# Last key chunk times values on 64x64 tiles, results by head, in a fused attention and mixer kernel

## The chip, the cores and the metric

The kernel runs on one core of a Trainium2 chip. The metric is the device time of one execution in microseconds. Before the change it is 580.24 us (median of three runs, 580.22 to 580.52).

## The reference, cut to what matters

```python
q_n = q / (norm(q) + 1e-6); k_n = k / (norm(k) + 1e-6)      # (8, 12, 448, 64)
scores = q_n @ k_n^T / tau                                   # tau = 0.1
attn = exp(scores) / sum(exp(scores))
x = (attn @ v), heads side by side                           # (8, 448, 768)
u = x + V^T (U^T x)                                          # rank 32, over the sequence
out = u + relu(u @ w_ch1) @ w_ch2                            # 768 -> 3072 -> 768
```

## The kernel before

Two heads form a pair, two pairs a couple; pair n = 6 b + p. Keys come in three chunks of 128 and a last one of 64. The last chunks of both heads of a pair share one tile of 128 rows. From n = 14 the kernel is in its steady state. A list of channel-mixer steps of the batch before ("fill") is spread between the parts of attention, so that TensorE (PE) never runs dry. One step is six matmuls, 0.98 us (second matrix, 384 columns) or 1.13 us (first matrix, 448 columns).

The product of the softmax numerators with the values, for half of the queries and both heads:

```python
def pe_V(b, p, half, bank):
    ...
    for i in range(2):                        # last chunk: both heads at once, 130 columns
        ic = 2 * half + i
        nc.tensor.matmul(out=av[:, i, :, :], lhsT=last_of(b, p)[:, ic * 128:(ic + 1) * 128],
                         rhs=vv[:, 2 * j:2 * j + 2, 3, :], start=(i == 0), stop=False, ...)
    for i in range(2):                        # three full chunks, head by head, 65 columns
        for h in range(2):
            for c in range(3):
                nc.tensor.matmul(out=av[:, i, h, :], lhsT=e[:, 2 * c + h, ...], rhs=vv[:, 2 * j + h, c, :], ...)
```

In the 130-column matmuls half of the products are with zeros: each head has its 64 keys in one half of the rows, and its values are zero in the other. Column 65 of the values is ones and gives the sum for the division on VectorE.

The steady loop (conditions that matter only outside it are left out), one turn for an even pair, one for the odd pair behind it; the number ahead of each part is its share of the fill put behind it:

```python
order = [                                                    # even n
    (2, lambda: (step_S3(*pairs[n]), Sc(n, 0, 1))),          # last-chunk scores of n and n+1, then chunks 0, 1
    (2, lambda: V(n - 1, 0)),
    (2, lambda: (V(n - 1, 1), X2(n - 1))),                   # X2: transposed copy of X by DMA
    (2, None),
    (3, lambda: (A2(n - 2), Sc(n, 2), Sc(n + 1, 0))),        # A2: U^T X of the couple n-2, n-1
    (2, False),
]
...
Sc(n, 1, 2)                                                  # odd n
H2(n - 3)                                                    # V (U^T X), added to the transposed X
...
order = [(2, lambda: V(n - 1, 0)), (2, None), (2, lambda: (V(n - 1, 1), X2(n - 1))), (2, None), (2, None)]
```

The result banks are two, `ps_av` and `ps_x`; the channel mixer has two more, `ps_m`, and the scores four: eight in all.

Of the kernel before, what the change touches and what calls it, by code (L numbers as in the profile page):

```python
# [9 lines left out]
FP = mybir.dt.float32  # L10
BF = mybir.dt.bfloat16
# [11 lines left out]
def kernel(  # L23
# [17 lines left out]
    nc = tc.nc  # L41

    B, H, S, D = q.shape
# [3 lines left out]
    NP = H // 2  # L47
    CC = C // 128
    NC = F // 128
    HC = C // 2  # L50
# [3 lines left out]
    work = ctx.enter_context(tc.tile_pool(name="work", bufs=2))  # L54
    psum = ctx.enter_context(tc.tile_pool(name="psum", bufs=1, space=bass.MemoryType.PSUM))
# [29 lines left out]
    est = Estimate()  # L85
# [24 lines left out]
    E, E3 = [], []  # L110
# [8 lines left out]
    def last_of(b, p):  # L119
        n = b * NP + p  # L120
        return E3[n // 2 % 2][:, n % 2, :]
# [63 lines left out]
    group_of = {}  # L185
# [30 lines left out]
    norm = {}  # L216
# [69 lines left out]
    FIRST4 = 2 * NP + 2  # L286
# [76 lines left out]

    X_of, av_of, A_of, up_of, XT_of = {}, {}, {}, {}, {}

    def pe_V(b, p, half, bank):
        gi, j = group_of[(b, p)]
        vv = norm[gi][1]
        e = E[(b * NP + p) % 2]
        if half == 0:  # L370
            X_of[(b, p)] = work.tile([128, 4, 128], BF, name="X", tag="X", bufs=2)
        av_of[(b, p, half)] = bank
        av = bank[:, 0:4 * (D + 1)].rearrange("p (i h d) -> p i h d", i=2, h=2)
        for i in range(2):
            ic = 2 * half + i
            nc.tensor.matmul(out=av[:, i, :, :], lhsT=last_of(b, p)[:, ic * 128:(ic + 1) * 128],  # L376
                             rhs=vv[:, 2 * j:2 * j + 2, 3, :],
                             start=(i == 0), stop=False, skip_group_check=True)
        for i in range(2):
# [3 lines that stand above are left out]
                    nc.tensor.matmul(out=av[:, i, h, :],  # L383
                                     lhsT=e[:, 2 * c + h, ic * 128:(ic + 1) * 128],
                                     rhs=vv[:, 2 * j + h, c, :],
                                     start=False, stop=(i == 1 and h == 1 and c == 2),
                                     skip_group_check=True)
        est.pe(0.52)
# [10 lines left out]
        est.dve(0.6)  # L399

    def step_V(b, p, half):
        if half == 1 and b * NP + p >= FIRST2:
            bank = psum.tile([128, 512], FP, name="up", tag="ps_x", bufs=1)
        else:
            bank = psum.tile([128, 512], FP, name="av", tag="ps_av", bufs=1)
        pe_V(b, p, half, bank)
        divide_V(b, p, half)
# [52 lines left out]
        XT_of[(b, p)] = t  # L460
        nc.sync.dma_start_transpose(out=t, in_=X_of[(b, p)].rearrange("p c d -> p (c d)"))

    def step_A2(b, p):
        ap = av_of[(b, p + 1, 1)][:, 384:512]
        for c in (0, 2):
            for i in range(2):
                for k in range(2):
                    r0 = 64 * i + 32 * k
                    nc.tensor.matmul(out=ap[r0:r0 + R, :], lhsT=U_sb[:, c + k, 0:R],  # L469
                                     rhs=X_of[(b, p + i)][:, c + k, :],  # L470
                                     start=False, stop=(c == 2), skip_group_check=True)
        A_of[(b, p)] = A_sb[(p // 2) % 2]
        nc.scalar.copy(out=A_of[(b, p)], in_=ap)  # L473
        est.pe(0.2)
        est.act(0.3)
# [16 lines left out]


    ut_of = {}

    def turn(b, half):

# [8 lines left out]
    def steps_m1(b):  # L506
        u = u_of(b)
        o = 64 if b % 2 == 0 else 0

        def one(f):  # L510
            mp = psum.tile([128, S], FP, name="mp", tag="ps_m", bufs=2)
            for cc in range(CC):
                nc.tensor.matmul(out=mp, lhsT=w1_sb[:, cc, f * 128:(f + 1) * 128],  # L513
                                 rhs=u[:, cc, 0:S], start=(cc == 0), stop=(cc == CC - 1))
            est.pe(1.13)
            if state_of["busy"] or est.act_first(0.55, 0.62):
                nc.scalar.activation(out=relu[:, f, o:o + S], in_=mp, func=AF.Relu)  # L517
            else:
                nc.vector.tensor_scalar_max(out=relu[:, f, o:o + S], in0=mp, scalar1=0.0)  # L519
            if b > 0 and f in (3, 12):  # L520
                turn(b, f // 12)

        return [lambda f=f: one(f) for f in range(NC)]

    def steps_m2(b):
        u = u_of(b)
        if b % 2 == 0:
            chunks = [(64 + 128 * c, 128 * c, c) for c in range(3)]
        else:
            chunks = [(384, 384, 3)] + [(128 * c, 128 * c, c) for c in range(3)]  # L530
        steps = []
        state = {}

        def part(half, ci, lo, hi, c0=0, c1=HC):
            r0, u0, c = chunks[ci]
            if lo == 0:
                state["mp"] = psum.tile([128, HC], FP, name="mp", tag="ps_m", bufs=2)
            mp = state["mp"][:, c0:c1]
            for f in range(lo, hi):
                nc.tensor.matmul(out=mp, lhsT=relu[:, f, r0:r0 + 128],  # L540
                                 rhs=w2_sb[:, f, half * HC + c0:half * HC + c1],
                                 start=(f == 0), stop=(b > 0 and f == NC - 1), skip_group_check=True)
            est.pe(0.0004 * (c1 - c0 + 6) * (hi - lo))
            if hi < NC:
                return
            o = work.tile([128, HC], FP, name="o_sb", tag="o_sb", bufs=3)[:, c0:c1]
            if b == 0:
                for i in range(3):
                    cc = half * 3 + i
                    nc.tensor.matmul(out=mp[:, i * 128:(i + 1) * 128], lhsT=u[:, cc, u0:u0 + 128],  # L550
                                     rhs=ident, start=False, stop=(i == 2), skip_group_check=True)
                est.pe(0.17)
                if est.act_first(0.48, 0.55):
                    nc.scalar.copy(out=o, in_=mp)
                else:
                    nc.vector.tensor_copy(out=o, in_=mp)
            else:
                nc.vector.tensor_add(o.rearrange("p (k d) -> p k d", d=128),  # L558
                                     mp.rearrange("p (k d) -> p k d", d=128),
                                     ut_of[(b, half)][:, c0 // 128:c1 // 128, c, :])  # L560
                est.dve(0.55)
            cols = slice(half * HC + c0, half * HC + c1)
            t4 = out[b, 0:256, cols].rearrange("(p c) d -> c p d", c=4)
            nc.sync.dma_start(out=t4[c], in_=o[0:64, :])
            if c < 3:
                t3 = out[b, 256:448, cols].rearrange("(p c) d -> c p d", c=3)
                other = nc.scalar if b == B - 1 and half == 1 else nc.sync
                other.dma_start(out=t3[c], in_=o[64:128, :])
            else:
                t4e = out[b - 1, 0:256, cols].rearrange("(p c) d -> c p d", c=4)  # L570
                nc.sync.dma_start(out=t4e[3], in_=o[64:128, :])

        for half in range(2):
            for ci in range(len(chunks)):
                if (b, half, ci) == (B - 1, 1, len(chunks) - 1):

                    for cs in ((0, 256), (256, 384)):
                        for i in range(2):
                            steps.append(lambda half=half, ci=ci, i=i, cs=cs:
                                         part(half, ci, 12 * i, 12 * i + 12, *cs))  # L580
                    continue
                for i in range(4):
                    steps.append(lambda half=half, ci=ci, i=i: part(half, ci, 6 * i, 6 * i + 6))
        return steps
# [4 lines left out]
    fill = []  # L589
# [22 lines left out]
    def Sc(n, *cs):  # L612
        step_S(*pairs[n], cs)

    def V(n, half):
        step_V(*pairs[n], half)
# [23 lines left out]
        M004 A5 red4q Ac5.a XT5 M104 H5 U5.a M045 M145 M205 red4k root4 M056 M156 R0 inv4 sc6q.v sc6k.v  # L640
        R1 M256 M306 R2 R3
    """
    bank1 = psum.tile([128, 512], FP, name="mp", tag="ps_m", bufs=2)
    spare = psum.tile([128, 512], FP, name="mp", tag="ps_m", bufs=2)
    copies = {"a": nc.scalar.copy, "v": nc.vector.tensor_copy}
    QK = {"q": 0, "k": 1}

# [149 lines left out]
    KEEP = 3  # L797
    for n in range(NP, NPAIR + 1):
# [38 lines left out]
        def X2(m):  # L837
            step_XT(*pairs[m])

        def A2(m):  # L840
            step_A2(*pairs[m])

        def H2(m):
            step_H2(*pairs[m])

        if n % 2 == 0:
            order = [
                (2, now and (lambda: (n >= FIRST4 and step_S3(*pairs[n]), Sc(n, 0, 1)))),
# [17 lines left out]
        if p == 1 and n - 2 > FIRST2:  # L866
            f(len(fill))
            fill.extend(steps_m1(b - 1) + steps_m2(b - 1))
        order = [
            (2, lambda: V(n - 1, 0)),  # L870
            (2, None if n > FIRST4 else (lambda: Sc(n, 3))),
            (2, lambda: (V(n - 1, 1), X2(n - 1))),
            (2, None),
            (2, None),
        ]
# [40 lines left out]
```

## Time and profile before

| | before |
|---|---|
| time | 580.24 us |
| span of the profiled run | 577.7 us |
| PE busy / chain of work that ended last | 98% / PE 95% |
| from the first last-chunk scores of n = 14 to the end ("the stretch") | 456.01 us |

The lines that carry the argument stand in the prediction. Most useful is a reading that no single view prints: the distance from one matmul's start to the next one's start. The ends of matmuls are modelled and overlap, but the starts add up to the time exactly.

### The profile page before, as it was taken

To read this page: it belongs to the slowest core of one execution; us is meant where nothing else is said; L and a number is where in the kernel's file an instruction comes from. 1 tells how busy PE (TensorE), PEld (TensorE's weight loads), DVE (VectorE), ACT (ScalarE), POOL (GpSimd) and SP (SyncE) were. 2 spreads that over 40 slices of the span, in tenths; PEclk is the share of its full clock that TensorE was granted. 3 is DMA by queue.
4 is the path that set the end of the run, shared out by engine and by line. 5 is a ranking of instruction groups with operands and counts; after the bars stand their busy time and mean duration, and the time that the engine had idled before them with its cause. 6 is when DMAs were issued, how large, how long until landed. Compare 5 with 4: busy or idle time off the path is not lost.

```text
span 577.7 us, 12301 instructions
## 1 busy us (share of the span) xinstructions
PE 568.7 (98%) x5098; PEld 329.3 (57%) x5098; DVE 211.8 (37%) x460; ACT 261.9 (45%) x449; POOL 213.8 (37%) x202
## 2 busy tenths in 40 slices
PE   7999999999999999999999999999999999999997
PEld 6665566555565556555555555655566555655565
DVE  6874552333342334423324333432244332320011
ACT  4877544555424653445324555246433374214300
POOL 8756574714416336416055064253261420000000
PEclk9999999999999999999999999999999999999999
DMA  6899999677467376575365663773654640231022
GB/s 166 192 249 239 235 209 213 181 144 138 104 149 176 81 142 136 134 142 111 91 159 146 113 137 99 148 174 83 128 131 113 132 74 16 54 71 36 6 50 57
DMA packets 139881, 74.52 MB, mean 129 GB/s; under 512 B 86688, under 2 KB 139696, under 8 KB 139824
## 3 DMA queue, kind: packets, MB, share of 16 engines
q1 hardware_dynamic: 129568, 63.20, 50.4%
q0 software_dynamic: 9632, 10.01, 10.2%
q8 instruction: 40, 0.66, 0.5%
q10 hardware_dynamic: 624, 0.51, 0.3%
q14 instruction: 17, 0.14, 0.1%
HBM read 52.19 MB, written 11.01 MB: 109 GB/s over the span
## 4 chain that ended last, share of the span: by engine, by line
PE 95%; DVE 1%; ACT 1%; SPq 1%; DMA 1%; issue 0%; DVEq 0%; ACTq 0%
PE mp L540 39%; PE mp L513 37%; PE sc L331 6%; PE av L383 3%; PE up L383 2%; PE av L376 1%; PE av L343 1%; PE tp L300 1%; PE sc L655 1%; PE up L376 1%; PE up L469 1%; DMA qst<-in_q_dram 1%; PE av L483 1%; ACT E L356 0%; PE sc L324 0%
## 5 line engine op out<-in xcount | busy, mean ns | idle before, releaser
L540 PE MATMUL mp<-w_sb,relu 128*128 128x384 bf16 (+2 forms) x1368 | 233.7, 323 | 0.0
L540 PEld LDWEIGHTS <-relu 128*128 128x128 bf16 x1368 | 126.7, 98 | 88.4 <-issue 13.1
L513 PEld LDWEIGHTS <-w_sb 128*128 128x128 bf16 x1128 | 105.1, 98 | 99.1 <-issue 9.7
L517 ACT ACTIVATE relu<-mp 128x448 bf16<-128x448 f32 x163 | 88.6, 543 | 128.3 <-PE mp L513 128.3
L356 ACT ACTIVATE E<-sc 128x896 bf16<-128x896 f32 x144 | 125.2, 923 | 21.7 <-PE sc L331 20.6
L268 POOL TENSOR_TENSOR qk<-kst,inv 128x512 bf16<-128x512 f32 x43 | 46.0, 1069 | 236.9 <-DVE inv L262 229.8
L513 PE MATMUL mp<-uO,w_sb 128*128 128x448 bf16 x576 | 114.2, 352 | 0.0
L513 PE MATMUL mp<-uE,w_sb 128*128 128x448 bf16 x552 | 112.9, 353 | 0.0
L558 DVE TENSOR_TENSOR o_sb<-mp,ut 128x384 f32<-128x384 f32 (+2 forms) x51 | 28.0, 549 | 141.0 <-PE mp L540 141.0
L248 DVE TENSOR_REDUCE ss<-sq 128x16 f32<-128x1024 f32 (+1 forms) x50 | 57.7, 1165 | 1.6 <-ACT sq L240 1.1
L268 POOL TENSOR_TENSOR qk<-qst,inv 128x512 bf16<-128x512 f32 x44 | 47.3, 1077 | 2.1 <-PE up L441 2.1
L383 PEld LDWEIGHTS <-E 128*128 128x128 bf16 x1152 | 45.0, 97 | 0.0
L519 DVE TENSOR_SCALAR relu<-mp 128x448 bf16<-128x448 f32 x25 | 15.6, 625 | 76.3 <-PE mp L513 75.8
L331 PE MATMUL sc<-qkT 64*64 64x448 bf16 x576 | 42.3, 359 | 0.6 <-ACT E L356 0.3
L243 POOL TENSOR_TENSOR sq<-kst 128x1024 f32<-128x1024 f32 (+1 forms) x23 | 42.6, 1855 | 0.2
L243 POOL TENSOR_TENSOR sq<-qst 128x1024 f32<-128x1024 f32 x21 | 39.9, 1899 | 7.3 <-DMA qst<-in_q_dram 7.3
L353 ACT ACTIVATE E<-av 128x448 bf16<-128x448 f32 x17 | 9.2, 541 | 47.3 <-PE up L343 47.3
L276 POOL CAST v<-vst 128x1024 bf16<-128x1024 f32 (+1 forms) x25 | 25.0, 1004 | 11.8 <-DMA vst<-in_v_dram 11.7
L383 PE MATMUL av<-v,E 128*128 128x65 bf16 x624 | 28.0, 193 | 0.0
L394 DVE RECIPROCAL rd<-av 128x4 f32<-128x4 f32 x52 | 9.3, 178 | 48.3 <-PE av L383 48.3
L473 ACT CAST A_sb<-up 128x128 bf16<-128x128 f32 x19 | 5.0, 263 | 47.6 <-PE up L469 47.6
L376 PEld LDWEIGHTS <-E 128*128 128x128 bf16 x192 | 18.0, 98 | 14.5 <-issue 0.8
(97 smaller groups left out, 347.8 us busy)
## 6 DMA issues: line engine op xcount, KB each, us to landing
out_dram<-o_sb SPq DMA_DIRECT2D x108, 96.0 KB, 2.2
w_sb<-in_moe_w_ch_dram POOLq DMA_DIRECT2D x8, 1152.0 KB, 18.4
qst<-in_q_dram SPq DMA_DIRECT2D x23, 256.0 KB, 3.9
vst<-in_v_dram SPq DMA_DIRECT2D x46, 128.0 KB, 3.0
kst<-in_k_dram SPq DMA_DIRECT2D x44, 128.0 KB, 2.8
qst<-in_q_dram SPq DMA_DIRECT2D x23, 192.0 KB, 3.9
vst<-in_v_dram SPq DMA_DIRECT2D x46, 96.0 KB, 2.8
kst<-in_k_dram SPq DMA_DIRECT2D x44, 96.0 KB, 2.7
```

The source lines that it names most:

```text
L243: nc.gpsimd.tensor_mul(sq[:, 0:self.nh * 4, :], self.flat(t), self.flat(t))
L248: nc.vector.reduce_sum(self.ss[:, j, 0:self.nh * 4], self.sq[j][:, 0:self.nh * 4, :], axis=AX.X)
L268: eng.tensor_mul(qks[self.gi % 2][:, j, i, :, :, :], t[:, 2 * j:2 * j + 2, :, :].rearrange("p h c d -> p c h d"), iv.unsqueeze(3).to_broad ...
L276: nc.gpsimd.tensor_copy(out=self.flat(v65[self.s])[:, :, 0:D], in_=self.flat(vst[self.s]))
L331: nc.tensor.matmul(out=sc[o:o + 64, h, 0:S], lhsT=t[r, 1, c * 128 + o:c * 128 + o + 64], rhs=t[r, 0, 0:S], start=True, stop=True)
L356: nc.scalar.activation(out=e[:, 2 * c:2 * c + 2, 0:S], in_=sc[:, :, 0:S], func=AF.Exp)
L376: nc.tensor.matmul(out=av[:, i, :, :], lhsT=last_of(b, p)[:, ic * 128:(ic + 1) * 128], rhs=vv[:, 2 * j:2 * j + 2, 3, :], start=(i == 0), s ...
L383: nc.tensor.matmul(out=av[:, i, h, :], lhsT=e[:, 2 * c + h, ic * 128:(ic + 1) * 128], rhs=vv[:, 2 * j + h, c, :], start=False, stop=(i == ...
L513: nc.tensor.matmul(out=mp, lhsT=w1_sb[:, cc, f * 128:(f + 1) * 128], rhs=u[:, cc, 0:S], start=(cc == 0), stop=(cc == CC - 1))
L517: nc.scalar.activation(out=relu[:, f, o:o + S], in_=mp, func=AF.Relu)
L540: nc.tensor.matmul(out=mp, lhsT=relu[:, f, r0:r0 + 128], rhs=w2_sb[:, f, half * HC + c0:half * HC + c1], start=(f == 0), stop=(b > 0 and f ...
L558: nc.vector.tensor_add(o.rearrange("p (k d) -> p k d", d=128), mp.rearrange("p (k d) -> p k d", d=128), ut_of[(b, half)][:, c0 // 128:c1 / ...
```

## The change

The intent: for even pairs, do the last chunk on four 64x64 tiles at once (two heads x two halves of each 128 queries), directly behind scores that use the same division of TensorE into tiles (the same "mode"). Results are kept by head, one bank each; the prediction says why. Both result banks are then taken at once, so U^T X moves to a bank of the channel mixer, and the even pair's products move up by a turn.

```diff
+    def open_V(b, p):
+        for h, (nm, tag) in enumerate((("av", "ps_av"), ("up", "ps_x"))):
+            av_of[(b, p, h)] = psum.tile([128, 512], FP, name=nm, tag=tag, bufs=1)
+        for ic in range(4):
+            for h in range(2):
+                r = slice(64 * h, 64 * h + 64)
+                for o in (0, 64):
+                    q0 = ic * 128 + o
+                    nc.tensor.matmul(out=av_of[(b, p, h)][o:o + 64, ic * (D + 1):(ic + 1) * (D + 1)],
+                                     lhsT=last_of(b, p)[r, q0:q0 + 64], rhs=vv[r, 2 * j + h, 3, :], ...)
+    def close_V(b, p, h):      # the 12 full-chunk products of one head, then its division
...
-        ap = av_of[(b, p + 1, 1)][:, 384:512]
+        ap = own_bank()[:, 0:128] if apart else av_of[(b, p + 1, 1)][:, 384:512]
...
+        if n % 2 == 0 and now and n >= FIRST4:
+            order = [
+                (3, lambda: (step_S3(*pairs[n]), Sc(n, 0, 1))),
+                (2, lambda: V(n - 1, 0)),
+                (3, lambda: (V(n - 1, 1), X2(n - 1))),
+                (4, lambda: (A2(n - 2), Sc(n, 2), Sc(n + 1, 0), open_V(*pairs[n]))),
+                (2, lambda: V(n, 0)),
+                (3, lambda: (V(n, 1), X2(n))),
+            ]
...                            # odd n: V(n - 1, 0), V(n - 1, 1), X2(n - 1) fall away
```

## The prediction

> **What bounds the kernel now.** I read the page's first two parts, then the groups with shapes kept apart, then the timeline of one couple of head pairs (n = 30, 31), then the list of who waited for whom.
>
> ```profile
> PE 568.7 (98%) x5098; PEld 329.3 (57%) x5098; DVE 211.8 (37%) x460; ACT 261.9 (45%) x449; POOL 213.8 (37%) x202
> PE   7999999999999999999999999999999999999997
> PEclk9999999999999999999999999999999999999999
> PE 95%; DVE 1%; ACT 1%; SPq 1%; DMA 1%; issue 0%; DVEq 0%; ACTq 0%
> ```
>
> TensorE (PE) is busy everywhere but in the first and last of 40 slices, at full clock, and is 95% of the chain that ended last. Busy alone is no proof (ends of matmuls are modelled), so I took the distance from each matmul's start to the next one's and sorted the distances by the pair of lines. After 120 us, where the changed stretch begins, they are almost constants: 162 ns for each 384-column matmul of the channel mixer (L540), 189 for each 448-column one (L513), 29 to 35 for the 65-column ones (L383); the worst outlier is 23 ns. PE therefore waits for nothing there: its own instruction stream is the time, and a nanosecond removed from it, or a wait added to it, counts in full.
>
> The timeline of the stretch that the change touches, PE alone (start, duration, engine, line):
>
> ```profile
> 304.24 0.28 PE L376 MATMUL av<-v,E 128*128 128x130 bf16 x2
> 304.36 0.54 PE L383 MATMUL av<-v,E 128*128 128x65 bf16 x12
> 304.74 2.11 PE L540 MATMUL mp<-w_sb,relu 128*128 128x384 bf16 x12
> ...
> 307.19 3.09 PE L540 MATMUL mp<-w_sb,relu 128*128 128x384 bf16 x18
> 310.21 0.30 PE L469 MATMUL up<-X,U_sb 128*32 128x128 bf16 x8
> 310.43 0.57 PE L331 MATMUL sc<-qkT 64*64 64x448 bf16 x8
> 310.94 0.34 PE L540 MATMUL mp<-w_sb,relu 128*128 128x384 bf16 x1
> ```
>
> Take starts, not durations: the two L376 matmuls (last key chunk, both heads, 130 columns) hold PE from 304.24 to 304.36, 0.12 us; twelve L383 take 0.38. The tiled work is in the last lines: L469 (128x32 tiles) 0.22 us, then eight score matmuls in two waves of four tiles, 0.51 us up to the next full-array matmul.
>
> **What the Trainium skill says.** "TensorEngine Tiling (Array Packing)", Tiling Modes, Key Properties: changing the tiling mode drains TensorE, while tiles of one mode run independently. The trace agrees. Within a mode a wave of 448-column scores follows the former after 179 ns; from scores to a full-array matmul the last start is followed after 282, so 95 to 105 ns extra, and from L540 into a tiled mode 256 instead of 162. The page's Restrictions say that column tiling disables Fast Weight Load. The trace shows the loads of a second wave 29 ns behind the first for 64 columns (15 ns for L469's 32 columns), so a 64-column load holds its tile about as long as 65 columns stream. "PSUM — Partial Sum Buffer", section "PSUM bank collisions raise a hardware error", says that row tiles may not write one bank at once but column tiles may: hence one head (one row tile) per bank. No run here shows a collision. "TensorE: Matmul & The Clock Gate", Part 3, The mechanism: loads are pulled ahead of matmuls in flight, and matmuls stay in order; in the trace, four loads stand before each second wave.
>
> **The change part by part.** It touches the even pairs n = 14, 16, ..., 46: 17 of them.
>
> Removed: four L376 matmuls per even pair, 17 x 4 = 68. By starts 61 + 58 ns per half, 119, twice: 238 ns per pair.
>
> Added: sixteen 64x64 matmuls of 65 columns, four waves of four tiles, put behind eight score matmuls that are in the same mode, so without a switch of their own. Before, the last score start was followed by the filler after 282 ns. Now: 179 to the first wave; 3 steps between waves of r; about 10 ns across the last wave's four starts; then the drain, estimated as 282 less the columns that are missing, (448 - 65)/2.4 = 160, so 122 (check: L469, 128 columns, leaves its mode after 149; less 63 columns = 26 gives 123). Sum 311 + 3r - 282 = 29 + 3r. I put r at 32 ns: L383, also 65 columns with a new weight tile each, repeats every 32, and neither the load (29) nor the stream (27) is longer. So 125 ns added.
>
> Net 238 - 125 = 113 ns per even pair, 17 x 113 = 1.9 us.
>
> Moved: the even pair's other 12 + 12 matmuls go from the odd iteration into the even one, one head per bank. Same count, 32 ns each: 0. The division remains two reciprocals and two multiplies over 128x4 and 128x256. Switches of mode per couple remain as they were. U^T X gets a channel bank because both result banks are now taken right behind it; its eight matmuls are the same, and their bank was released a step earlier. 0, if it comes to no wait.
>
> **The wait I expect.** The 17 parts of an iteration are filled with 7 or 9 steps of channel work. Before, three such steps stood between the odd pair's second half and U^T X, which reads that half's X. Now there are two with 9 steps and one with 7. X is ready 0.84 to 1.50 us after PE's next instruction; worst where a reduction and the eviction of a channel group stand in VectorE's queue (n = 24, 36):
>
> ```profile
> 371.33 1.21 DVE L248 TENSOR_REDUCE ss<-sq 128x16 f32<-128x1024 f32 x1
> 372.45 0.55 DVE L558 TENSOR_TENSOR o_sb<-mp,ut 128x384 f32<-128x384 f32 x1
> 372.92 0.17 DVE L394 RECIPROCAL rd<-up 128x4 f32<-128x4 f32 x1
> 373.12 0.42 DVE L395 TENSOR_TENSOR X<-up,rd 128x256 bf16<-128x256 f32 x1
> ...
> 371.66 0.54 PE L383 MATMUL up<-v,E 128*128 128x65 bf16 x12
> 372.04 3.09 PE L540 MATMUL mp<-w_sb,relu 128*128 128x384 bf16 x18
> 375.06 0.30 PE L469 MATMUL up<-X,U_sb 128*32 128x128 bf16 x8
> ```
>
> Here 18 L540 matmuls hide it. With six, the second wave of U^T X would be due at 372.04 + 0.98 + 0.09 + 0.07 = 373.18, but X is there at 373.54 plus some 0.06 for the signal: 0.42 us of wait. At n = 22 and 34 (X after 1.08, due 1.14) it just fits; at 20, 32, 44 the step is a 1.13 us one and X comes after 0.92. So 2 x 0.42 = 0.85 us.
>
> Sum: 580.24 - 1.92 + 0.85 = 579.2 us.
>
> **The rivals.**
> (a) No wait: the scheduling order hides it all. For it: only two of 17 places are tight by the trace. Against: the order of VectorE's instructions in the changed program is the same there, reduce, eviction, division. It makes 578.3.
> (b) Loads bound the small waves: without Fast Weight Load, load and stream follow each other instead of overlapping, r about 60. For it: no stretch of before has more than two or three tiled waves in a row, and none so short. Against: loads of the next wave stand 2 ns behind the matmuls of the last one. Then 29 + 180 = 209 added, 29 ns won per pair, 0.5 us; with the waits 580.6.
> (c) The softmax becomes the bound: the even pair's product now follows its third score chunk after one or two steps. Before, the exponentials end 1.35 to 1.40 us after that chunk's first score matmul (310.43 to about 311.8). Now the third matmul of the product needs it, at 0.62 for scores and small tiles + 0.98 for a step + 0.06 = 1.66. 0.2 us are left, so no wait, but if the relus shift on ScalarE this could cost 0.2 us at each of eight pairs, 1.6 us: 580.8.
> (d) The transposed copy of X now asks for its buffer before the couple before has used it, so the DMA queue waits 2 to 3 us for VectorE. What stands behind it, the transposes of the next couple, has some 8 to 10 us until its use and lands in a median of 3.7. Hidden: 0.
>
> **Range and chances.** The gain is a sum of counted instructions with r the only estimate in it: r from 29 to 40 moves the sum by -0.15 to +0.4 us. Waits are 0 (a) to 2.5 (c with mine). Runs of before lie within 0.3 us. I put 8 in 10 on 578.0 to 580.4. 2% is 11.6 us, six times the whole gain and far above any wait that I found: faster 0.01, same 0.98, slower 0.01.
>
> **What would show it.** The L376 group falls from 192 to 124 instructions and a new one of 272 on 64x64 tiles appears, waves 29 to 36 ns apart (right) or about 60 (rival b). From last score to filler: about 311 + 3r ns. The list of waits names the X multiply as releaser of U^T X at two places with about 0.4 us each; none elsewhere means (a). A wait of the first-chunk products for the exponentials means (c). PE's full-array distances stay 162, 189, 32. The prediction is wrong if PE shows waits that I did not name, or if leaving the small-tile mode costs more than 122 ns.

## The result, and the profile after

The changed kernel takes 579.98 us (median of four runs, 579.48 to 580.29), the kernel before 580.23 beside it (four runs). The ratio is 0.9996, interval 0.9979 to 1.0014: no difference can be told.

From the page of the changed kernel, engine shares and the chain that ended last:

```profile
PE 567.5 (98%) x5302; PEld 330.3 (57%) x5302; DVE 212.9 (37%) x460; ACT 262.6 (45%) x449; POOL 214.0 (37%) x202
...
PE 83%; DMA 8%; DVE 3%; SPq 2%; POOL 1%; ACT 1%; issue 1%; POOLq 0%; DVEq 0%
```

Busy PE still reads 98%, and says nothing of what follows. Its chain fell from 95% to 83%, and DMA rose in it from 1% to 8%. That is no measure of the waits below either: three DMA pieces ahead of 80 us make up 40 us of it, and e3, which loses its waits further down, still has 7%.

To see where, start distances are summed by kind of matmul, each distance given to the matmul that opens it, from the first last-chunk scores of n = 14 to the end ("the stretch"). Up to there the parts of attention stand in the same order in both programs. Two columns belong to experiments further down.

| us, start to next start | before | changed | e3 both edits | e7 full array |
|---|---|---|---|---|
| 130-column matmuls (L376; L412) | 8.35 | 4.29 | 4.29 | 8.35 |
| 16 small tiles x 17 (L378) | 0 | 3.92 | 3.92 | 0 |
| scores of chunks 0 to 2 (L331) | 23.61 | 22.34 | 21.86 | 23.60 |
| last-chunk scores (L343) | 3.62 | 4.33 | 3.63 | 3.63 |
| U^T X (L469; L508) | 4.08 | 4.93 | 4.07 | 4.07 |
| 65-column products (L383; L393, L419) | 26.48 | 26.52 | 26.52 | 26.45 |
| channel mixer | 380.73 | 380.73 | 380.73 | 380.71 |
| the rest, with the tail | 9.16 | 9.22 | 9.16 | 9.17 |
| sum | 456.01 | 456.29 | 454.18 | 455.98 |

The gain is there: 130-column matmuls -4.06, the scores -1.75 in the version without waits (their last start is followed after 179 ns by a wave in the same mode, no longer after 282 by a full-array matmul), the small tiles +3.92: 1.89 us won. It went again in two places: U^T X +0.85, and the two kinds of scores together +1.18 against that version (0.48 + 0.70). The stretch is 0.28 us longer than before. The rest of the difference of the two profiled spans (578.5 and 577.7) lies ahead of n = 14, which starts at 122.23 us here and at 121.67 before. The nine profiles, one of each kernel, have it anywhere from 121.5 to 123.6, and runs of the kernel before scatter by 2.0 us, so whole times say little here. The stretches of e7 and of the kernel before, neither of which waits, agree to 0.03.

**The first wait, U^T X.** Timeline of the changed kernel at n = 36, PE and VectorE lines kept:

```profile
371.85 0.54 PE L419 MATMUL up<-v,E 128*128 128x65 bf16 x12
372.23 1.14 PE L598 MATMUL mp<-w_sb,relu 128*128 128x384 bf16 x6
372.64 0.55 DVE L617 TENSOR_TENSOR o_sb<-mp,ut 128x384 f32<-128x384 f32 x1
...
373.30 0.29 PE L508 MATMUL mp<-X,U_sb 128*32 128x128 bf16 x6
373.31 0.42 DVE L431 TENSOR_TENSOR X<-up,rd 128x256 bf16<-128x256 f32 x1
...
373.79 0.23 PE L508 MATMUL mp<-X,U_sb 128*32 128x128 bf16 x2 [0.20 <-DVE X L431]
373.95 0.57 PE L331 MATMUL sc<-qkT 64*64 64x448 bf16 x8
374.35 0.19 PE L378 MATMUL av<-v,E 64*64 64x65 bf16 x2
...
374.58 1.15 PE L598 MATMUL mp<-w_sb,relu 128*128 128x384 bf16 x6
```

One step (six L598) stands between the odd pair's second half and U^T X, where the kernel before had eighteen matmuls. Six of the eight U^T X matmuls go at 373.30 to 373.36; the last two need X's second half, whose multiply ends at 373.73, and start at 373.79. By starts the seventh matmul comes 422 ns behind the sixth where 3 is usual, so 0.42 us are lost. The bracket says only 0.20, since it counts from the modelled end of the matmul before. The same 0.42 stands at n = 24, nowhere else; the two make up the 0.85 of the table's row but for 0.01.

**The second wait, the last-chunk scores.** Changed kernel, n = 42 (PE's four matmuls L343 are two for the even pair into `av` and two for the odd into `up`; SPq lines are the DMA queue issuing transfers):

```profile
430.61 0.62 DVE L528 TENSOR_TENSOR uE<-av,XT 128x448 bf16<-128x448 f32 x1
...
431.26 2.00 SPq L500 DMA_TRANSPOSE XT<-X  x1
433.30 0.59 SPq L623 DMA_DIRECT2D out_dram<-o_sb  x1
433.93 0.59 SPq L627 DMA_DIRECT2D out_dram<-o_sb  x1
...
434.64 2.65 SPq L315 DMA_TRANSPOSE qkT<-qk  x2
...
438.41 0.38 PE L343 MATMUL av<-qkT 64*64 64x448 bf16 x2
...
439.22 0.38 PE L343 MATMUL up<-qkT 64*64 64x448 bf16 x2 [0.43 <-DMA qkT<-qk]
```

The kernel before at the same place:

```profile
429.32 0.63 DVE L488 TENSOR_TENSOR uE<-av,XT 128x448 bf16<-128x448 f32 x1
...
430.62 2.69 SPq L315 DMA_TRANSPOSE qkT<-qk  x2
...
436.48 1.23 SPq L461 DMA_TRANSPOSE XT<-X  x1
...
438.12 0.38 PE L343 MATMUL av<-qkT 64*64 64x448 bf16 x2
438.12 0.38 PE L343 MATMUL up<-qkT 64*64 64x448 bf16 x2
```

In the changed kernel the transposed copy of X (L500) is asked for before the couple before has used its buffer (L528). The queue issues in order, so it stands still until 431.26, and the transposes of the next couple (L315) behind it are issued at 434.64 instead of 430.62. The second of them lands at 439.17, read from its landing event; the odd pair's scores start right then, 0.81 us behind the even pair's instead of 0.01. The same costs 0.29 us at n = 30 and 0.08 at n = 18.

Why these three: at the first couple of each batch (n = 18, 24, 30, 36, 42) the copy's issue starts 7.15 us ahead of the scores. At n = 42 it is then 2.04 us until the next issue, two stores of results (L623, L627) 1.34, and the transposes 4.53 until the second has landed: 7.91 us, 0.76 too much. At n = 24 and 36 no store stands between, and they land 0.28 and 0.82 us in time.

### The profile page after: what moved, and what is told of

Read it like the earlier page. It is cut to its first block, busy times and chain, and to the rows that moved or that the text cites. A ratio compares the mean times of both kernels' runs of the same rounds, so it can differ in the third digit from the quotient of the medians.

```text
span 578.5 us, 12651 instructions
## 1 busy us (share of the span) xinstructions
PE 567.5 (98%) x5302; PEld 330.3 (57%) x5302; DVE 212.9 (37%) x460; ACT 262.6 (45%) x449; POOL 214.0 (37%) x202
## 4 chain that ended last, share of the span: by engine, by line
PE 83%; DMA 8%; DVE 3%; SPq 2%; POOL 1%; ACT 1%; issue 1%; POOLq 0%; DVEq 0%
PE mp L598 34%; PE mp L570 33%; PE sc L331 5%; DMA w_sb<-in_moe_w_ch_dram 5%; DMA kst<-in_k_dram 2%; PE av L419 2%; PE up L419 1%; PE av L393 1%; PE up L393 1%; PE av L343 1%; POOL sq L243 1%; SPq L315 1%; PE mp L508 1%; ACT E L356 1%; DVE ss L248 1%
## 5 line engine op out<-in xcount | busy, mean ns | idle before, releaser
L598 PE MATMUL mp<-w_sb,relu 128*128 128x384 bf16 (+2 forms) x1368 | 235.3, 323 | 0.3 <-DMA w_sb<-in_moe_w_ch_dram 0.3
L598 PEld LDWEIGHTS <-relu 128*128 128x128 bf16 x1368 | 126.1, 98 | 84.1 <-issue 9.6
L331 PE MATMUL sc<-qkT 64*64 64x448 bf16 x576 | 42.8, 360 | 0.6 <-ACT E L356 0.3
L419 PEld LDWEIGHTS <-E 128*128 128x128 bf16 x744 | 29.1, 97 | 0.0
L331 PEld LDWEIGHTS <-qkT 64*64 64x64 bf16 x576 | 12.8, 105 | 14.2 <-issue 8.6
L393 PEld LDWEIGHTS <-E 128*128 128x128 bf16 x408 | 17.3, 97 | 5.0
L419 PE MATMUL av<-v,E 128*128 128x65 bf16 x420 | 18.9, 193 | 0.0
L412 PEld LDWEIGHTS <-E 128*128 128x128 bf16 x124 | 11.4, 98 | 9.0 <-issue 0.8
```

The lines of the kernel that those rows point to most:

```text
L331: nc.tensor.matmul(out=sc[o:o + 64, h, 0:S], lhsT=t[r, 1, c * 128 + o:c * 128 + o + 64], rhs=t[r, 0, 0:S], start=True, stop=True)
L393: nc.tensor.matmul(out=av[:, ic, :], lhsT=e[:, 2 * c + h, ic * 128:(ic + 1) * 128], rhs=vv[:, 2 * j + h, c, :], start=False, stop=(ic == 3 ...
L419: nc.tensor.matmul(out=av[:, i, h, :], lhsT=e[:, 2 * c + h, ic * 128:(ic + 1) * 128], rhs=vv[:, 2 * j + h, c, :], start=False, stop=(i == ...
L598: nc.tensor.matmul(out=mp, lhsT=relu[:, f, r0:r0 + 128], rhs=w2_sb[:, f, half * HC + c0:half * HC + c1], start=(f == 0), stop=(b > 0 and f ...
```

## The experiments

Theory T: the small tiles win about 0.11 us at each of 17 pairs; the two waits of the schedule give it back, one by VectorE's order, one by the order in the DMA queue. Rival R1: small matmuls win nothing, and all differences are schedule. Rival R2: the waits have other causes (crowded DMA engines, the channel bank), so the edits would not remove them. A first attempt at the DMA wait, a third buffer for the transposed copy, did not fit into SBUF (the pool wanted 31.6 KB per partition, 30.6 were left); e1 changes the order instead. Kernels e1 to e4 ran on one chip beside the kernel before, with 579.94 us median of eleven runs (579.24 to 581.21); e5 to e7 were added later; the 579.88 of their twelve runs of before counts the same eleven and one more. All results were correct.

**e1: the copy of X behind the next couple's transposes.**

```diff
-                (3, lambda: (V(n, 1), X2(n))),
+                (3, lambda: V(n, 1)),
...  # odd n, behind H2(n - 3) and the transposes of the next couple
+        if n > FIRST4:
+            X2(n - 1)
```

> The even pair's transposed copy of X is asked for after U^T X V of the couple before and behind the transposes of the next couple, as in the kernel before; nothing else changes. Theory (the DMA queue stands still behind that copy, so the next couple's transposes land too late at n = 18, 30, 42): the three waits inside the last-chunk scores (0.07, 0.30, 0.81 us in the changed kernel's trace) go, the transposes are issued 2 to 4 us sooner against these scores; from the first last-chunk scores (n = 14) to the end 456.29 - 1.17 = 455.1 us, whole time about 578.8. The waits of U^T X at n = 24 and 36 (0.42 us by starts) stay. Rival (the transposes are late because PE is ahead or the DMA engines are crowded): the waits stay, 456.3 us.

Measured: 578.91 us median of five (578.38 to 579.54), ratio 0.9982 (0.9971 to 0.9994); the stretch is 455.07 us. All three waits at the scores are gone. The timeline at n = 42:

```profile
431.88 3.43 SPq L315 DMA_TRANSPOSE qkT<-qk  x2
...
435.39 1.22 SPq L500 DMA_TRANSPOSE XT<-X  x1
...
438.51 0.38 PE L343 MATMUL av<-qkT 64*64 64x448 bf16 x2
438.52 0.38 PE L343 MATMUL up<-qkT 64*64 64x448 bf16 x2
```

The transposes are issued 6.6 us ahead of the scores instead of 3.8, and nothing waits. Here the second one lands 1.2 us ahead, so the reserve is small still. U^T X keeps its 0.85 us (4.94 us by starts). T holds for the DMA wait, R2 falls for it.

**e2: both reductions ahead of the odd pair's divisions.**

```diff
-            at = [(m - 3, 0), (m - 3, 0), (m - 3, 5)] + [(m - 2, i) for i in (0, 1, 2)]
+            at = [(m - 3, 0), (m - 3, 0), (m - 3, 5)] + [(m - 2, i) for i in (0, 0, 2)]
```

> Both reductions of a couple's squares are put in VectorE's queue right after the last-chunk scores, ahead of the odd pair's divisions; nothing else changes. Theory (U^T X waits at n = 24 and 36 because a reduction and an eviction stand before the division): these two waits, 0.42 us by starts where 0.056 is usual, go; 456.29 - 0.73 = 455.6 us from n = 14 to the end, whole time about 579.2; the waits for the transposes at n = 18, 30, 42 stay or shrink a little. Rival (the wait is for the channel bank or for ScalarE): 456.3 us and the two waits stay.

Measured: 579.10 us median of six (578.28 to 580.36), ratio 0.9985 (0.9973 to 0.9997); stretch 454.97, a little shorter than expected: the waits at the scores were 0.02, 0.31 and 0.42 us in this profile instead of 0.08, 0.29 and 0.81 (0.43 less in all), and U^T X gave back 0.86 us and not 0.73 (the expectation took 56 ns, the distance between the two waves, for the usual one; it is 3 ns). The timeline at n = 36:

```profile
371.06 1.14 PE L598 MATMUL mp<-w_sb,relu 128*128 128x384 bf16 x6
...
371.47 0.42 DVE L431 TENSOR_TENSOR X<-up,rd 128x256 bf16<-128x256 f32 x1
...
372.12 0.29 PE L508 MATMUL mp<-X,U_sb 128*32 128x128 bf16 x8
```

X is ready at 371.89, before U^T X starts, and all eight matmuls go in one group; the longest distance within U^T X is 57 ns. T holds for this wait too.

**e3: both edits.**

> Both edits together. Theory: no wait is left on PE but those of before; the 17 pairs give 17 x 107 = 1.8 us; 456.29 - 1.17 - 0.73 = 454.4 us from n = 14 to the end against 456.01 in the kernel before, whole time about 578.2, ratio to before 0.9965. Rival (something else gives the gain back): no faster than before, ratio 0.999 or more.

Measured: 578.31 us median of six (577.53 to 579.74), ratio 0.9976 (0.9963 to 0.9990); stretch 454.18, so 1.83 us below the kernel before. In its table column every row but the three of the change agrees with before to 0.04 us. The expected ratio, 0.9965, lies inside the interval. The profiled run (579.63) is one of the two slowest of the six: it reached n = 14 only at 123.63 us, and its list of waits names 1.2 and 0.6 us for the weights' DMA on PE, with no such entry before. This version is faster than the kernel before, and by its stretch than the changed one, by an amount far below the 2% that would be called faster.

**e4: the changed schedule, the last chunk on the full array.**

```diff
-                (4, lambda: (A2(n - 2), Sc(n, 2), Sc(n + 1, 0), open_V(*pairs[n]))),
+                (4, lambda: (A2(n - 2), Sc(n, 2), Sc(n + 1, 0))),
```

(The even pair's product then falls back to the routine of before, by half.)

> The schedule, the banks and the channel bank for U^T X of the changed kernel, but the even pairs' last key chunk is multiplied on the full array in 130-column matmuls as before, results by half. Theory (the small tiles save 107 ns at each of 17 pairs and the new waits come from the schedule): the waits stay, 456.29 + 1.82 = 458.1 us from n = 14 to the end, whole time about 581.8. Rival (the tiles save nothing, all is schedule): 456.3 us.

Measured: 581.55 us median of four (581.09 to 581.65), ratio 1.0026 (1.0011 to 1.0040); stretch 457.41 instead of 458.1. The waits at the scores were smaller here, 0.53 us in all (0.44, 0.03, 0.07), where the changed kernel had 1.17. Without them the two stretches are 456.88 and 455.12, 1.76 us apart. R1 falls: without the small tiles the change is a loss.

**e5: the small tiles away from the scores**, from e3.

```diff
-                (4, lambda: (A2(n - 2), Sc(n, 2), Sc(n + 1, 0), open_V(*pairs[n]))),
-                (2, lambda: V(n, 0)),
+                (4, lambda: (A2(n - 2), Sc(n, 2), Sc(n + 1, 0))),
+                (2, lambda: (open_V(*pairs[n]), V(n, 0))),
```

> From the version with both edits (454.18 us from n = 14 to the end): the sixteen small matmuls are not put behind the scores but just before the even pair's other products, between full-array matmuls, so with two changes of mode of their own. Theory (what counts is the place next to the scores): entering costs 256 instead of 162 ns to the first wave and some 24 more until its weights are in, then 3 x 29.5 + 10 + 127: 343 ns a pair where behind the scores it is 122; 17 x 221 = 3.8 us more, 457.9 us, whole time about 582.1, more than before. Rival (changes of mode are hidden, the tiles save by themselves): 454.2 us.

Measured: 581.70 us median of four (581.50 to 581.97), ratio 1.0031 (1.0016 to 1.0045); stretch 458.11. PE's timeline:

```profile
425.29 2.12 PE L598 MATMUL mp<-w_sb,relu 128*128 128x384 bf16 x12
427.35 0.22 PE L378 MATMUL av<-v,E 64*64 64x65 bf16 x2
...
427.47 0.20 PE L378 MATMUL up<-v,E 64*64 64x65 bf16 x2
427.60 0.55 PE L393 MATMUL av<-v,E 128*128 128x65 bf16 x12
```

The same sixteen matmuls, their starts spread over 0.13 us instead of 0.10, but entered 256 ns behind a full-array matmul instead of 162 (283 instead of 189 where it has 448 columns), and followed again by one after 127. The scores again pay 282 instead of 179 to leave their mode. That is 3.93 us more than e3, and 2.13 more than doing the chunk on the full array in the same schedule (e7 below). The gain is not the small tiles; it is small tiles where the mode is open already.

**e6: U^T X back in the result bank**, from e3.

```diff
-            step_A2(*pairs[m], now and m + 2 >= FIRST4)
+            step_A2(*pairs[m], False)
```

> From the version with both edits: U^T X goes into the unused columns of the odd pair's second result bank as before, not into a channel bank. Theory (that bank is wanted again 0.61 us after U^T X starts, and ScalarE's copy out of it ends 0.6 us after the start, 0.8 where a relu stands before it): waits at the first small matmul of the second bank, about 0.07 us at 11 pairs and 0.25 at 6, 1.5 to 2.5 us in all, 455.7 to 456.7 us. Rival (the bank was never wanted): 454.2 us.

Measured: 580.11 us median of four (579.78 to 580.63), ratio 1.0004 (0.9991 to 1.0017); stretch 456.25. The timeline shows what the second bank waits for:

```profile
334.53 0.26 ACT L513 CAST A_sb<-up 128x128 bf16<-128x128 f32 x1
334.61 0.19 PE L378 MATMUL av<-v,E 64*64 64x65 bf16 x2
...
334.84 0.22 PE L378 MATMUL up<-v,E 64*64 64x65 bf16 x2
```

The first matmul of `up` follows 227 ns behind the second of `av` at six pairs, where a relu stands ahead of the copy on ScalarE, and 33 at the other eleven; 4 is usual. At all seventeen it starts 52 ns behind the copy's end. The stretch is 2.07 us longer than e3's. So the third part of the change, the channel bank, is needed: without it the gain is gone.

**e7: e3 with the last chunk on the full array.**

> From the version with both edits: the last key chunk of the even pairs on the full array, 130 columns, by half; no waits. Theory (the tiles alone give 238 - 122 = 116 ns a pair, 2.0 us, or 107, 1.8, by the totals): 456.0 to 456.2 us, as the kernel before (456.01), no wait at the scores or at U^T X; whole time about 580.2. Rival (the reordering itself gains or loses): a different stretch from before's by over 0.3 us.

Measured: 579.91 us median of four (579.56 to 580.75), ratio 1.0002 (0.9989 to 1.0014); stretch 455.98 against 456.01 before. The reordering itself costs and brings nothing once the waits are out, and what small tiles bring is e7 less e3: 1.80 us, 106 ns a pair.

## Why the prediction was right or wrong

The number was right: 579.98 lies in the range, and it was clear that no 2% were to be had. Step by step:

- **Removed, 238 ns a pair**: right. 4.06 us over 17 pairs are 239.
- **Added, 125 ns a pair**: the small tiles hold PE 3.92 us, 231 ns a pair, less 103 for the scores that they follow: 128. The waves repeat every 31 ns (prediction 32), and leaving the mode costs 127 instead of the estimated 122. Rival (b), waves of 60 ns, is out.
- **Net 113 ns, 1.9 us**: measured 106 to 108 ns, 1.80 (e7 less e3) or 1.83 us (before less e3). The mechanism and nearly the size.
- **Its signs of being wrong**: two came true. Leaving the mode cost more than 122 ns, by 5 ns, 0.09 us in all; and PE shows waits that it did not name (rival d).
- **U^T X waits 0.42 us at n = 24 and 36, nowhere else, 0.85 in all**: right in place, cause and size; the row is 0.85 us longer, and e2 takes it out by moving the reduction that was named.
- **Rival (c)**, waits for the exponentials: none; the 65-column rows agree to 0.04 us.
- **Rival (d)**, "Hidden: 0": wrong. This is the step that failed. The queue does stand still, by 2.0 to 2.4 us at the three couples that lost time (the prediction gave 2 to 3), but the copy's own issue comes on top, the pair of transposes takes 4.5 us from the first issue to the second landing (n = 42) and not the 3.7 of one, and "some 8 to 10 us until its use" was read at one couple, n = 32. Taken for all, the reserve in the kernel before, from the second landing to the scores, is 1.4 to 8.6 us. At n = 18, 30 and 42 it is 1.65, 2.44 and 2.83, and the landing moved against the scores by 1.69, 2.69 and 3.60: 1.18 us lost. The smallest reserve, 1.40 at n = 36, was not used up; there the landing moved by 0.58. So a table of all landings against all uses, from the trace that was at hand, would have shown how thin the reserve was, and the delay of each place had to be set against it.
- **The sum**: 580.24 - 1.92 + 0.85 missed +1.18 of DMA wait and about 0.1 us of gain (a few ns at each pair). By the stretch, the change is +0.28 us where -1.07 was forecast. That the whole time lies in the range is partly luck: the range, 578.0 to 580.4, took in no change at all, and the runs of one kernel scatter by more than what was missed.

What stays open: the wait at n = 42 was 0.81, 0.42 and 0.07 us in three profiles with the same order in the queue (changed, e2, e4). It goes with the copy's issue, which took 2.00, 1.58 and 1.22 us; what held that issue was not tried. Each stretch is read from one profile. Nor was the scatter ahead of n = 14 taken apart.

## What to carry to other kernels

Small matmuls on tiles pay where the mode is open already: behind work in the same tiling sixteen of them cost 128 ns where the full-array form costs 239; between full-array matmuls they cost 125 more than it (2.13 us over 17 pairs). When a bound engine has no wait at all, every reordering has to be checked place by place: list, for all repetitions, when each input is ready, when it is used and by how much the change delays it, and look at the place where the delay is largest against the reserve, not at a typical one. An in-order DMA queue passes a wait for a buffer on to everything behind it, so a transfer whose buffer is not free yet belongs behind those that are urgent.

## What the Trainium skill lacked or had wrong

- "TensorEngine Tiling (Array Packing)", Tiling Modes, Key Properties, says that a change of mode drains TensorE, without a figure. Here a change costs 94 to 103 ns: 256 instead of 162 on entering, 282 instead of 179 after 448-column scores, 127 after a wave of 65 columns where the next wave comes after 31.
- "TensorE: Matmul & The Clock Gate", Part 2, LDWEIGHTS, gives P / 1.2 ns for P columns, so 53 ns for 64. Here waves that each load 64 columns into four tiles repeat every 31 ns, and the loads of a second wave stand 29 ns behind the first for 64 columns and 15 for 32. As a spacing of loads that is about half of the figure, at least for tiles; how long one load really lasts is not shown (its records read 92 to 107 ns).
- The same page, Part 3, The mechanism, says that loads overlap matmuls in flight only when the row group differs. Here the next full-array load stands 2 ns behind the start of a full-array matmul (162 ns apart, all rows the same), so that list is too narrow. Part 2 and the paragraph ahead of it in the same section also allow a background weight buffer.
- "Perfetto Trace Analysis", Tensor Engine Instruction, says that a matmul's end is estimated, but neither it nor another page says that the idle time ahead of a matmul therefore understates a wait: it shows 0.20 us for U^T X at n = 36, where starts show 0.42 lost.
